# Projections beside PV issued as four column groups in one transformer layer

## The chip, the core and the metric

The kernel runs on one core of one Trainium2 chip. The metric is the device time of the kernel in microseconds (us), as the median of several runs. A difference is told against the kernel before, in per cent. The core has a matrix engine (PE, whose weight loads the profile lists apart as PEld), an elementwise engine (DVE), an activation engine (ACT), a general engine (POOL), a queue engine (SP) and 16 DMA engines. They run side by side and wait for each other through semaphores.

## The reference

One layer of 2048 rows and width 1024: an attention block with 32 query heads of 32 columns that share one key head and one value head, and a gated feed-forward block of width 3584. Each block stands behind a layer norm and is added to its input. All data are bf16.

```python
def attention(x, wq, wk, wv, wo):            # S = 2048, D = 1024, 32 heads of 32
    q = (x @ wq).reshape(B, S, 32, 32).transpose(0, 2, 1, 3)
    k, v = x @ wk, x @ wv                    # 32 columns each, shared by all heads
    p = softmax(einsum("bhqd,bkd->bhqk", q, k) * 32 ** -0.5)
    return einsum("bhqk,bkd->bhqd", p, v).transpose(0, 2, 1, 3).reshape(B, S, D) @ wo

def feed_forward(x, w_gate, w_up, w_down):   # F = 3584
    return (sigmoid(x @ w_gate) * (x @ w_up)) @ w_down

h = x + attention(layernorm(x), wq, wk, wv, wo)
out = h + feed_forward(layernorm(h), w_gate, w_up, w_down)
```

## The kernel before

**Three kinds of work on PE, three tilings of its array.** A score burst ("S", lines 685 and 695) multiplies keys by queries. The contraction is only 32 long, so four matmuls stand side by side in four row groups of the array (`tile_position=(DH * j, 0)`, form 32*128 in the profile). PV (line 842 for most of the run, 965 and 968 in the first chunk) multiplies the values by the exponentials. The stationary operand has only 32 columns, so four matmuls stand side by side in four column groups (`tile_position=(0, DH * j)`, form 128*32). The sums of the exponentials over the keys (lines 881, 894 and 947) have the tiling of PV, with ones as weights. Everything else uses the whole array (form 128*128): the Q, K and V projections and the output projection (`mm_list`, line 334), gate and up (`half_items`, line 1180) and down (`down_group`, line 1250). The document calls this third kind "f", as the code does (`kind="f"`), and calls a run of one kind between two others a stretch.

**The bursts.** Rows come in 16 tiles of 128, two tiles make a unit, and there are 8 units. The attention of a row tile is cut into quads (`ORDER`), and each quad into 8 bursts. In all there are `NB` = 512 bursts. A burst fills four banks of PSUM, and ACT empties them with two exponentials of 128x1024. Three pairs of banks (`S_ps`) are passed around. The other two banks (`X_ps`) take everything else, one group at a time in each: a group of PV has 8 items, each of four matmuls with 512 columns, and a group of f has as many items as its sum has terms. For every two groups of PV there is a group of sums with one item (`sum_group`, held in `pv_follow` until it is taken up).

**Who sets the order.** The program is written out by a planner in Python. It keeps a clock for each engine (`k_pe` and others), adds to it an estimated cost for each instruction and `T_SW` = 0.1 whenever the kind of work changes (`mode`), and picks the next item from the loop at the end of the kernel. In this order: a burst, if its banks are free by the planner's clock (`due`); an item of a PV group that has been started; output projections that are urgent; a new PV group, if its exponentials have been issued (`pv_ready`) and a burst was just made; else an item of the current f group (`cur`). So the time between two bursts, a gap, is filled with PV and f. The table `PV_PLAN` has a letter for each of the 64 quads: `a` puts off the start of a PV group while the current f group has under 1.0 left; `c` and `e` start it behind the next burst; `d` and `e` let a burst wait for the end of a PV group; a capital takes up the group of sums at once. Where the next item of PV waits for an exponential, the loop takes an item of f instead if the wait is over 0.25 by the clock (`2.5 * T_SW`, when the last kind was PV) or over 0.02 (otherwise).

**The f groups by size.** Gate and up take the weights as stationary operand and the rows as moving operand: 256 rows when both tiles of a unit are ready, 128 when only the first is (`first_tile`, whose second tile follows as a step of its own, for which the weights are loaded once more unless they are held). Down, the output projection and most of Q have 512 columns. The weights of gate and up are streamed from memory for each unit into the slots of `halves`, by SP's queue.

**Before the main loop.** A written-out head (`HEAD`) covers the first 72 us with the first projections and the first PV groups. The change is switched on where the loop starts.

Of the kernel before, what the change touches and what calls it, by code (L numbers as in the profile page):

```python
# [12 lines left out]
P = 128  # L13
DH = 32
# [70 lines left out]
def bass_sequential_preLN__grouped_kv_mqa__glu_gated_glu__prompt_kernel(  # L85
# [15 lines left out]
    DT = D // P  # L101
    NT = S // P
    KT = S // P
    NQ = D // P
    QC = 256
    NQC = S // QC
    TPQ = QC // P
    NFT = F // P
# [3 lines left out]
    BPG = KT // 2  # L112
    NB = NQC * NQ * BPG
# [2 lines left out]
    HR = 4  # L116
    NGU = 4
    NEAR = 1
    PV_PLAN = "aaaaAeAaaeaaaeaAaebabaaAdaddaaaAdababaaadabadaaCdabadaaEcaaaacaa"
    WO_PLAN = "aaaaaaba"  # L120
    PV_HOLD = 1.0
    BANK_WAIT = 0.15
# [11 lines left out]
    T_MM, T_FIX, T_SW, T_EXP, T_TANH, T_ADD = 0.0004167, 0.00267, 0.1, 0.91, 0.48, 0.61  # L134
# [4 lines left out]
    with ExitStack() as es:  # L139
# [6 lines left out]
        QT = sb("QT", [NQ, S])  # L146
# [26 lines left out]
        k_pe, k_dve, k_act, k_pool, k_sp, k_dma = [0.0], [0.0], [0.0], [0.0], [0.0], [0.0]  # L173
# [8 lines left out]
        c_pool, c_s, c_e, c_pv = ctr("c_pool", k_pool), ctr("c_s", k_pe), ctr("c_e", k_act), ctr("c_pv", k_pe)  # L182
# [18 lines left out]
        wd = zv(0, [NFT, D])  # L201
# [22 lines left out]
        hact = hact_flat[:].rearrange("p (a b) -> p a b", a=NFT)  # L224
# [14 lines left out]
        def _(unused):  # L239
# [48 lines left out]
            pe_mode = [None]  # L288

            def mode(m):  # L290
                if pe_mode[0] != m:
                    k_pe[0] += T_SW
                    pe_mode[0] = m
# [5 lines left out]
            def open_group(g):  # L299
# [3 lines left out]
                need(pe, f(True) if callable(f) else f)  # L303
                bank_free[b] = "open"

            def run_item(g):
                if g.bank is None:
                    need(pe, *[v() if callable(v) else v for v in g.after])
                    open_group(g)
                mode(g.kind)  # L310
                fn = g.items.popleft()[1]
                tick = fn(X_ps[:, g.bank, :])
                if not g.items:
                    dve_fill(when(tick) + g.room)
                    bank_free[g.bank] = g.evac(X_ps[:, g.bank, :], tick)
# [12 lines left out]
            def mm_list(pairs, sel, n):  # L328

                items = []  # L330
                last = len(pairs) - 1
                for i, (a, b) in enumerate(pairs):
                    def f(bank, i=i, a=a, b=b):
                        ins = pe.matmul(sel(bank), lhsT=a, rhs=b, start=(i == 0), stop=(i == last))  # L334
                        return mm_done(ins, n, i == last)
                    items.append((n * T_MM + T_FIX, f))
                return items
# [338 lines left out]
            def s_burst(k):  # L676
                g, b = quad(k), burst(k)[2]
                t, i = ORDER[g]
                mode("s")
                need(pe, (c_e, 2 * k - 1) if k > 0 else None, k_val[key_tile(g, b) // 2 if wide(g) else b],  # L680
                     *q_ready(g), *(xnT_ready(0, 1) if k < 2 else ()))
                if wide(g):
                    kt = key_tile(g, b)
                    for j in range(4):
                        ins = pe.matmul(S_ps[:, ((2 * k + j // 2) % 3) * 2 + j % 2, :],  # L685
                                        lhsT=kT4[DH * j:DH * (j + 1), kt * P:(kt + 1) * P],
                                        rhs=QT[DH * j:DH * (j + 1), i // 2 * 4:i // 2 * 4 + 4, t * P:(t + 1) * P],
                                        start=True, stop=True, tile_position=(DH * j, 0))
                        if j % 2 == 1:
                            c_s.inc(ins, 0.109, 0.3)  # L690
                    return
                for kt in range(2):
                    for j in range(4):
                        bank = ((2 * k + j // 2) % 3) * 2 + j % 2
                        ins = pe.matmul(S_ps[:, bank, kt * QC:(kt + 1) * QC],  # L695
                                        lhsT=kT4[DH * j:DH * (j + 1), (2 * b + kt) * P:(2 * b + kt + 1) * P],
                                        rhs=QT[DH * j:DH * (j + 1), 2 * i:2 * i + 2, t * P:(t + 1) * P],
                                        start=True, stop=True, tile_position=(DH * j, 0))
                        if kt == 1 and j % 2 == 1:
                            c_s.inc(ins, 0.115, 0.3)  # L700
# [469 lines left out]
            def half_items(n, w):  # L1170
                c, ts, fs, _ = steps[n]
                us, r0, m = step_halves(n, w), ts[0] * P, len(ts) * P
                items = []
                for j in range(2 * len(fs)):
                    for dt in range(DT):
                        def f(bank, j=j, dt=dt):
                            u = us[j // 2]
                            i = half_at[u]
                            need(pe, half_val[u])
                            ins = pe.matmul(bank[:, j * m:(j + 1) * m], lhsT=halves[i][:, dt, j % 2 * P:(j % 2 + 1) * P],  # L1180
                                            rhs=QT[:, dt, r0:r0 + m], start=(dt == 0), stop=(dt == DT - 1))
                            tick = mm_done(ins, m, dt == DT - 1)
                            if j % 2 == 1 and dt == DT - 1:
                                if i > H_KT and not held(n):
                                    wd_free.append((ZONE[i - H_KT - 1], [tick]))
                                elif not held(n):
                                    half_free.append((i, [tick]))
                                if w == 1 and c < NU - 1 and j == 2 * len(fs) - 1 and ffn_list[0][0] == "down":
                                    half_free.append((4 + c, [tick]))
                                load_halves()  # L1190
                            return tick
                        items.append((m * T_MM + T_FIX, f))
                return items
# [49 lines left out]
            def down_group(c, tt, dc, lo=0, n=512):  # L1243
                t, c0 = UNITS[c][tt], dc * 512 + lo
                items = []
                for ft in range(NFT):
                    def f(bank, ft=ft):
                        f1 = ft | 1
                        need(pe, hact_val[(t, f1)])
                        ins = pe.matmul(bank[:, 0:n], lhsT=hact[:, ft, tt * P:(tt + 1) * P],  # L1250
                                        rhs=wd[:, ft, c0:c0 + n], start=(ft == 0), stop=(ft == NFT - 1))
                        return mm_done(ins, n, ft == NFT - 1)
                    items.append((n * T_MM + T_FIX, f))

                def evac(bank, tick):
                    i = oi[0]
                    oi[0] += 1
                    need(dve, tick)
                    hv = hx[:, t % HR, c0:c0 + n]
                    v = c_dve.inc(dve.scalar_tensor_tensor(out=hv, in0=bank[:, 0:n], scalar=0.5, in1=hv,  # L1260
                                                           op0=ALU.mult, op1=ALU.add), 0.03 + n * 0.00113, 0.08)
                    next_x()
                    need(sp, v)
                    o_val[i] = dma(sp, of[t * P:(t + 1) * P, c0:c0 + n], hv, d_o[t % HR])
                    if dc == DC - 1:
                        if t + HR < NT:
                            x_due.append((t, o_val[i]))
                        if t == UNITS[c][-1]:
                            down_last[c] = tick
                    return v  # L1270
                assert wd_next[0] == NFP
                return _Group(items, evac, [wd_val[0]])
# [14 lines left out]
            def busy(g):  # L1287
                return g is not None and bool(g.items)
# [224 lines left out]
                                B_w_down[2 * i * P:2 * (i + 1) * P, :].rearrange("(a p) n -> p a n", p=P), d_wd, 512)  # L1513


            urg = [None]
            since_s = [0.0]
            idle = 0
            while True:
# [35 lines left out]
                    continue  # L1555
                if busy(pv[0]):
                    t_ = pv[0].items[0][2]()
                    if t_ > k_pe[0] + (2.5 * T_SW if pe_mode[0] == "pv" else 0.02):
                        if not busy(cur[0]):
                            cur[0] = next_group()  # L1560
                        if busy(cur[0]):
                            run_item(cur[0])
                            continue
                        if t_ > k_pe[0] + 0.6 and can_s:
                            k_pe[0] += 0.05
                            dve_fill(k_pe[0])
                            continue
                    run_item(pv[0])
                    continue
# [88 lines left out]
```

## Time and profile before

| what | value |
|---|---|
| median of 3 runs | 1100.33 us (1098.34 to 1101.48) |
| the profiled execution | 1100.95 us, span 1098.9 us |
| granted clock of PE | 0.997 |
| PE, matmuls | 1082.9 us busy (99%), 11612 instructions |
| ACT | 1008.4 us busy (92%), 1155 instructions |
| DVE | 899.6 us busy (82%), 1496 instructions |
| DMA | 173.34 MB, SP's queue 57.4% of 16 engines' span |

"Busy" is the union of the durations of an engine's instructions. A matmul's duration holds its way through the array, so that matmuls overlap one another and a busy PE is not one at its peak: what a matmul costs in a stream is the distance from its start to the next one's start. The timeline merges neighbouring instructions of a line and a shape into one row with its start, its length to the end of the last one, and their count. The times of starts in it are therefore what to read.

### The profile page before, as it was taken

Reading aid. Unit: us, or ns where it says so; the run is one execution under the profiler, and the core shown is the slowest. Engines: PE = TensorE matmul, PEld = TensorE weight load, DVE = VectorE, ACT = ScalarE, POOL = GpSimd, SP = SyncE. Lnnn points to the kernel's source line nnn. Section 1 sums busy time; section 2 is a strip of 40 time slices with the busy share of each in tenths; the row PEclk is TensorE's granted clock in tenths of the full one; section 3 lists DMA queues with packets and bytes.
Section 4 is the critical chain, followed back from the end, with each engine's and each line's share of the span. In section 5 each row is a group of like instructions: output and inputs, shape, how many; then the busy total and the mean of one; then the engine's idle time right before and its main releaser. Section 6 shows DMA issues by size and latency. Waiting matters only on the chain.

```text
span 1098.9 us, 27392 instructions
## 1 busy us (share of the span) xinstructions
PE 1082.9 (99%) x11612; PEld 616.4 (56%) x11612; DVE 899.6 (82%) x1496; ACT 1008.4 (92%) x1155; POOL 64.5 (6%) x136
## 2 busy tenths in 40 slices
PE   7899999999999999999999999999999999999999
PEld 5554456643666346643666346653665446653884
DVE  7759998799988889799987989898988889798311
ACT  6899999999999999999999999999999999999110
POOL 4500110010000000000000000000000000000000
PEclk9899999999999999999999999999999999999999
DMA  9743318940966539670999419670585609881660
GB/s 218 141 119 108 106 52 249 260 137 20 253 201 187 124 103 253 197 202 20 238 245 246 112 29 269 195 182 30 143 241 155 145 20 277 221 232 35 149 175 20
DMA packets 328233, 173.34 MB, mean 158 GB/s; under 512 B 39472, under 2 KB 322352, under 8 KB 328112
## 3 DMA queue, kind: packets, MB, share of 16 engines
q1 hardware_dynamic: 322304, 161.37, 57.4%
q0 software_dynamic: 2544, 9.44, 2.5%
q8 instruction: 91, 1.49, 0.6%
q10 hardware_dynamic: 3264, 0.79, 0.4%
q14 instruction: 30, 0.25, 0.1%
HBM read 159.51 MB, written 4.19 MB: 149 GB/s over the span
## 4 chain that ended last, share of the span: by engine, by line
PE 95%; ACT 2%; DVE 1%; DMA 1%; POOL 1%; issue 0%; DVEq 0%; ACTq 0%
PE X_ps L1180 38%; PE X_ps L1250 19%; PE S_ps L685 13%; PE X_ps L334 10%; PE X_ps L842 10%; PE S_ps L695 1%; PE X_ps L968 1%; ACT Pr L718 1%; PE X_ps L881 1%; DVE st L381 1%; PE X_ps L965 1%; ACT hact L718 1%; DMA zone<-zone 0%; DMA hx<-in_A_x_dram 0%; POOL sd L360 0%
## 5 line engine op out<-in xcount | busy, mean ns | idle before, releaser
L718 ACT ACTIVATE Pr<-S_ps 128x1024 bf16<-128x1024 f32 x992 | 936.0, 1112 | 4.0 <-PE S_ps L695 1.6
L768 DVE TENSOR_TENSOR pairs<-Pr 128x1024 bf16<-128x1024 bf16 x446 | 303.6, 683 | 28.4 <-ACT Pr L718 27.7
L780 DVE TENSOR_TENSOR pairs<-pairs 128x1024 bf16<-128x1024 bf16 x390 | 268.9, 689 | 11.0
L1180 PE MATMUL X_ps<-QT,wgu 128*128 128x128 bf16 (+1 forms) x2656 | 257.7, 247 | 0.7 <-issue 0.6
L1180 PEld LDWEIGHTS X_ps<-QT,wgu 128*128 128x128 bf16 x2656 | 198.4, 98 | 54.0 <-issue 35.9
L1250 PE MATMUL X_ps<-zone,hact 128*128 128x512 bf16 (+2 forms) x924 | 216.9, 374 | 0.0
L685 PE MATMUL S_ps<-QT,kT 32*128 32x512 bf16 x1792 | 176.8, 385 | 0.0
L1180 PE MATMUL X_ps<-QT 128*128 128x128 bf16 (+1 forms) x1840 | 175.8, 245 | 0.6 <-issue 0.5
L1180 PEld LDWEIGHTS X_ps<-QT 128*128 128x128 bf16 x1840 | 136.5, 98 | 33.2 <-issue 21.3
L1250 PEld LDWEIGHTS X_ps<-zone,hact 128*128 128x128 bf16 x924 | 78.8, 98 | 104.4 <-issue 30.4
L1201 ACT ACTIVATE gu<-X_ps 128x512 f32<-128x512 f32 x112 | 78.3, 699 | 45.9 <-PE X_ps L1180 45.9
L1222 DVE SCALAR_TENSOR_TENSOR hact<-gu,X_ps 128x512 bf16<-128x512 f32 x112 | 76.5, 683 | 52.4 <-PE X_ps L1180 51.7
L685 PEld LDWEIGHTS S_ps<-QT,kT 32*128 32x128 bf16 x1792 | 45.1, 91 | 129.9 <-ACT Pr L718 114.3
L842 PE MATMUL X_ps<-Pr,V 128*32 128x512 bf16 x1792 | 114.7, 381 | 0.0
L334 PE MATMUL X_ps<-zone 128*128 128x512 bf16 (+3 forms) x576 | 78.3, 281 | 4.2 <-DMA zone<-zone 2.1
L842 PEld LDWEIGHTS X_ps<-Pr,V 128*32 128x32 bf16 x1792 | 40.2, 96 | 50.8 <-issue 16.8
L334 PE MATMUL X_ps<-wo,QT 128*128 128x512 bf16 x256 | 63.5, 381 | 0.0
L334 PEld LDWEIGHTS X_ps<-zone 128*128 128x128 bf16 x576 | 39.3, 99 | 33.5 <-issue 13.9
L349 POOL CAST mean<-mv 128x1 f32<-128x1 bf16 x28 | 8.7, 309 | 817.9 <-DVE mv L1093 802.9
L1260 DVE SCALAR_TENSOR_TENSOR hx<-X_ps,hx 128x512 bf16<-128x512 f32 (+2 forms) x33 | 22.2, 672 | 24.7 <-PE X_ps L1250 24.5
L903 DVE STREAM_TRANSPOSE ols<-X_ps 128x512 f32<-128x512 f32 x28 | 20.0, 716 | 23.0 <-PE X_ps L881 21.5
L334 PEld LDWEIGHTS X_ps<-wo,QT 128*128 128x128 bf16 x256 | 22.2, 98 | 28.9 <-issue 8.5
(94 smaller groups left out, 541.7 us busy)
## 6 DMA issues: line engine op xcount, KB each, us to landing
wgu<-in_B_w_up_dram SPq DMA_DIRECT2D x81, 512.0 KB, 5.7
wgu<-in_B_w_gate_dram SPq DMA_DIRECT2D x72, 512.0 KB, 5.5
QT<-in_B_w_gate_dram SPq DMA_DIRECT2D x55, 512.0 KB, 5.8
QT<-in_B_w_up_dram SPq DMA_DIRECT2D x46, 512.0 KB, 6.0
zone<-in_B_w_down_dram POOLq DMA_DIRECT2D x14, 512.0 KB, 5.6
out_dram<-hx SPq DMA_DIRECT2D x31, 128.0 KB, 1.7
hx<-in_A_x_dram SPq DMA_DIRECT2D x15, 256.0 KB, 2.7
Pr<-in_B_w_gate_dram SPq DMA_DIRECT2D x5, 512.0 KB, 6.9
```

Of the source, the lines that this page charges most:

```text
L334: ins = pe.matmul(sel(bank), lhsT=a, rhs=b, start=(i == 0), stop=(i == last))
L685: ins = pe.matmul(S_ps[:, ((2 * k + j // 2) % 3) * 2 + j % 2, :], lhsT=kT4[DH * j:DH * (j + 1), kt * P:(kt + 1) * P], rhs=QT[DH * j:DH * ( ...
L718: c_e.inc(act.activation(out=p_tile(k, n % 2), in_=S_ps[:, 2 * pr:2 * pr + 2, :].rearrange("p a (b q) -> p (a b) q", q=QC), func=ACTF.Exp, ...
L768: slot_use[x] = c_dve.inc(dve.tensor_tensor(out=dst(x), in0=p_tile(k - 1, hh), in1=p_tile(k, hh), op=ALU.add), T_ADD, 0.08)
L780: slot_use[x] = slot_use[y] = c_dve.inc(dve.tensor_tensor(out=pairs[:, x, :], in0=pairs[:, x, :], in1=pairs[:, y, :], op=ALU.add), T_ADD, ...
L842: ins = pe.matmul(bank[DH * j:DH * (j + 1), :], lhsT=V[:, kt, :], rhs=p_tile(k, j // 2)[:, j % 2 * 2:j % 2 * 2 + 2, :], start=b == 0, stop ...
L903: free = c_dve.inc(dve.transpose(ols[:], bank), 0.75, 0.08)
L1180: ins = pe.matmul(bank[:, j * m:(j + 1) * m], lhsT=halves[i][:, dt, j % 2 * P:(j % 2 + 1) * P], rhs=QT[:, dt, r0:r0 + m], start=(dt == 0), ...
L1201: tanh_val[n] = c_act.inc(act.activation(out=slot, in_=bank, func=ACTF.Tanh, scale=0.5), T_TANH, 0.1)
L1222: gu_read[n] = c_dve.inc(dve.scalar_tensor_tensor(out=hact[:, 2 * fs[0]:2 * fs[0] + ft, r0:r0 + len(ts) * P], in0=slot.rearrange("p (a b) ...
L1250: ins = pe.matmul(bank[:, 0:n], lhsT=hact[:, ft, tt * P:(tt + 1) * P], rhs=wd[:, ft, c0:c0 + n], start=(ft == 0), stop=(ft == NFT - 1))
L1260: v = c_dve.inc(dve.scalar_tensor_tensor(out=hv, in0=bank[:, 0:n], scalar=0.5, in1=hv, op0=ALU.mult, op1=ALU.add), 0.03 + n * 0.00113, 0.08)
```

## The change

Three edits go together.

The first is in `run_item`. Before an item of f is issued, a new function `by_columns` decides whether the item is written in PV's tiling. It does so in the main loop only. If the last kind on PE was PV, it says yes as long as there are bursts to come (or a PV group is under way, or a group of sums waits). If the last kind was a burst, it says yes when a PV group is under way, a group of sums waits, or the next PV group has its exponentials. If the last kind was f on the whole array, it says no. An item for which it says yes is counted by the planner as PV work (`mode("pv")`), and the new function `mm` issues four matmuls for it, each with 32 of the 128 weight columns, to 32 of the 128 partitions of the bank, with the same moving operand. `mm` takes the place of `pe.matmul` in `mm_list`, `half_items` and `down_group`.

The second is in the loop: the wait for an exponential beyond which an item of f is put between two items of PV is 0.02 in every case.

The third is in the tables: `PV_PLAN` has other letters, and the planner's cost of half a burst is 0.113 where it was 0.109.

```diff
-    PV_PLAN = "aaaaAeAaaeaaaeaAaebabaaAdaddaaaAdababaaadabadaaCdabadaaEcaaaacaa"
+    PV_PLAN = "aaacAaaaaacaadaDaaaaadaBaaaaaaaBaaaaaacBdacaaaaAdaabaaaAcababaaa"
...
+            main = [False]
+
+            def by_columns():
+                if not main[0]:
+                    return False
+                more = busy(pv[0]) or pv_follow[0] is not None
+                if pe_mode[0] == "pv":
+                    return more or k[0] < NB
+                n = pv_next[0]
+                return pe_mode[0] == "s" and (more or n < NQC * NQ and k[0] >= min(BPG * (n + 1) + 1, NB - (n == NQC * NQ - 1)))
+
+            def mm(out, lhsT, rhs, start, stop):
+                if pe_mode[0] != "pv":
+                    return pe.matmul(out, lhsT=lhsT, rhs=rhs, start=start, stop=stop, skip_group_check=main[0])
+                for j in range(4):
+                    ins = pe.matmul(out[DH * j:DH * (j + 1)], lhsT=lhsT[:, DH * j:DH * (j + 1)], rhs=rhs, start=start,
+                                    stop=stop, tile_position=(0, DH * j), skip_group_check=True)
+                return ins
...
-                mode(g.kind)
+                mode("pv" if g.kind == "f" and by_columns() else g.kind)
...
-                        ins = pe.matmul(sel(bank), lhsT=a, rhs=b, start=(i == 0), stop=(i == last))
+                        ins = mm(sel(bank), a, b, i == 0, i == last)
...
-                            c_s.inc(ins, 0.109, 0.3)
+                            c_s.inc(ins, 0.113, 0.3)
...
-                            ins = pe.matmul(bank[:, j * m:(j + 1) * m], lhsT=halves[i][:, dt, j % 2 * P:(j % 2 + 1) * P],
-                                            rhs=QT[:, dt, r0:r0 + m], start=(dt == 0), stop=(dt == DT - 1))
+                            ins = mm(bank[:, j * m:(j + 1) * m], halves[i][:, dt, j % 2 * P:(j % 2 + 1) * P],
+                                     QT[:, dt, r0:r0 + m], dt == 0, dt == DT - 1)
...
-                        ins = pe.matmul(bank[:, 0:n], lhsT=hact[:, ft, tt * P:(tt + 1) * P],
-                                        rhs=wd[:, ft, c0:c0 + n], start=(ft == 0), stop=(ft == NFT - 1))
+                        ins = mm(bank[:, 0:n], hact[:, ft, tt * P:(tt + 1) * P], wd[:, ft, c0:c0 + n],
+                                 ft == 0, ft == NFT - 1)
...
+            main[0] = True
...
-                    if t_ > k_pe[0] + (2.5 * T_SW if pe_mode[0] == "pv" else 0.02):
+                    if t_ > k_pe[0] + 0.02:
```

## Prediction

> **What bounds the kernel now.** I read the page first: busy shares, slices, chain.
>
> ```profile
> PE 1082.9 (99%) x11612; PEld 616.4 (56%) x11612; DVE 899.6 (82%) x1496; ACT 1008.4 (92%) x1155; POOL 64.5 (6%) x136
> ...
> PE   7899999999999999999999999999999999999999
> ...
> ACT  6899999999999999999999999999999999999110
> ...
> PE 95%; ACT 2%; DVE 1%; DMA 1%; POOL 1%; issue 0%; DVEq 0%; ACTq 0%
> ```
>
> PE is on the chain for 95% of the span. ACT is full too, but only to the 37th slice: the last exponential ends at 1015 us, and what follows is PE alone, as the chain in order of time shows:
>
> ```profile
> 1024.99 47.60 PE X_ps L1180 x608
> 1072.59 24.26 PE X_ps L1250 x140
> ```
>
> So ACT sets when the attention ends, and PE sets when the kernel ends: it has 83 us of f left by then. A microsecond of PE saved before 1015 us takes f out of this tail, if there is f to bring forward.
>
> Then the timeline of PE shows what PE loses. It hardly ever waits; it pays at every change of tiling.
>
> ```profile
> 329.53 0.40 PE L685 MATMUL S_ps<-QT,kT 32*128 32x512 bf16 x4
> 329.85 1.69 PE L842 MATMUL X_ps<-Pr,V 128*32 128x512 bf16 x28
> 331.48 0.39 PE L685 MATMUL S_ps<-QT,kT 32*128 32x512 bf16 x4
> 331.80 0.40 PE L842 MATMUL X_ps<-Pr,V 128*32 128x512 bf16 x4
> 332.14 1.16 PE L1180 MATMUL X_ps<-QT 128*128 128x256 bf16 x9
> 333.23 0.40 PE L685 MATMUL S_ps<-QT,kT 32*128 32x512 bf16 x4
> 333.55 0.94 PE L1180 MATMUL X_ps<-QT 128*128 128x256 bf16 x7
> 334.33 0.82 PE L1180 MATMUL X_ps<-QT,wgu 128*128 128x256 bf16 x6
> 335.08 0.40 PE L685 MATMUL S_ps<-QT,kT 32*128 32x512 bf16 x4
> 335.42 0.40 PE L881 MATMUL X_ps<-pairs,ones 128*32 128x512 bf16 x4
> 335.76 1.70 PE L1180 MATMUL X_ps<-QT,wgu 128*128 128x256 bf16 x14
> ```
>
> Read starts. Seven items of PV take from 329.85 to 331.48: seven times 0.216 (the stream's distance) and 0.12 for the change to S. The single PV item at 331.80 is followed by f 0.34 later, 0.12 more than its 0.216. Every burst is entered and left at such a price, and every meeting of PV and f costs one more.
>
> **The change, part by part.** *Meetings that go.* Counted along PE's timeline from 72 us, where the loop starts: 78 stretches go from PV to f, 34 from f to PV. One of the 78 lies behind the last burst and stays. By the new rule f behind PV, and f between a burst and PV, is in PV's tiling, so 77 and 34 meetings vanish. Prices are medians of starts less the stream's distance. PV to f costs 116 ns, and the f matmul behind it is followed 11 ns late. Against that, leaving column groups for a burst costs 106 ns, leaving f costs 96 (the four of a group start 3 ns apart). So one meeting is worth 116 + 11 - 10 = 117 ns, and 77 of them 9.0 us. Burst, f, PV, burst costs 122 + 104 + 106 at its three borders; burst, columns, burst costs 119 + 106; 34 x 107 ns = 3.6 us. Together 12.6 us. The 2 x 512 borders of bursts stay.
>
> *What the column form costs at each size.* Laid over the order of before, the rule takes 1050 items of f: those behind or ahead of PV in its gap, those of 26 gaps in which a group of sums waits, and those of 7 gaps in which PV was ready and put off. By columns moved they are 302 of 512 or 384, 564 of 256 and 184 of 128, some 137 us of f. For 512 the row is PV itself: 0.216 for four, as f's own 0.216 for one. Cost nothing. For 256 the first chunk's PV shows it:
>
> ```profile
> 68.06 0.28 PE L965 MATMUL X_ps<-Pr,ones 128*32 128x256 bf16 x4
> 68.17 0.28 PE L968 MATMUL X_ps<-Pr,V 128*32 128x256 bf16 x4
> 68.28 0.28 PE L965 MATMUL X_ps<-Pr,ones 128*32 128x256 bf16 x4
> 68.39 0.28 PE L968 MATMUL X_ps<-Pr,V 128*32 128x256 bf16 x4
> ```
>
> Four each 0.109, with four fresh weight loads; f at 256 columns also takes 0.109. Cost nothing. For 128 columns no row has the column form. On the whole array one takes 0.056:
>
> ```profile
> 966.21 0.62 PE L1180 MATMUL X_ps<-QT,wgu 128*128 128x128 bf16 x8
> 966.66 1.11 PE L1180 MATMUL X_ps<-QT 128*128 128x128 bf16 x17
> 967.71 0.39 PE L685 MATMUL S_ps<-QT,kT 32*128 32x512 bf16 x4
> ```
>
> (25 in 1.50, less 0.096 for the change.) In columns, four matmuls and four loads have to fit into that. Bounds: 56 ns, as the pace was the moving operand's at 512 and at 256; and 109 ns, the pace at 256, if there the loads and not the moving operand set it. In the raw starts at 256 each load follows its matmul by 2 ns and the next matmul by another 2, so eight instructions go in 12 ns; that is far nearer to 56. I take 56 and no cost, and keep 184 x 53 ns = 9.8 us as the other end. If f of 128 columns fell into column gaps by its share of all f (137 of 603 us; 2048 such items lie in the loop), 465 x 53 ns = 25 us.
>
> [...]
>
> *Instructions.* 1050 items become 4200 matmuls and as many loads, 6300 instructions more. The instruction queue's 91 packets carried 27392; some 21 more come, on a queue of 0.6%. I cost it at nothing, since PE has fetched 8 per 0.109 us from 66.96 to 71.7 us without a hole. If each new packet were waited for as long as the hole of 241 ns at 293.3 us, 5 us: kept for the range.
>
> *What PE does with the time.* It must find f sooner. The planner does a unit's gate and up on its first tile alone when PE is early: 2048 items of 128 columns over seven units, half of them first tiles, 146 a unit out of 448. Being early by another 12.6 us in the last unit needs 225 more: 371, still under 448. So the work is there. Its price: two items of 56 take 2.5 ns more than one of 109. Early by c/8 of 12.6 us in unit c sums to 44 us, 790 items: 2.0 us. Some 12 more pairs of weight blocks are loaded twice, 25 MB on 173; the queues would pass from 57% to 66% of the span, below the 80% that the busiest 100 us already hold (900 to 1000).
>
> *The wait of 0.02.* The old 0.25 made PE wait inside a PV group. From 72 us on PE's starts show four holes of over 60 ns between matmuls of one kind, 0.6 us in all, none of them in PV. Between nothing and 0.6 us gain; I take nothing.
>
> *The tables.* Letters and the burst's 0.113 only move stretches. Nothing on the chain is shorter or longer: bursts keep two borders whatever the letter. The seventh quad loses its capital: one more sum item, 0.11 us. Bounds ±1.2 us, ten meetings more or fewer than in the order of before. ACT's and DVE's instructions stay the same, and an item that delays a burst stays at most 0.216 long.
>
> Sum: -12.6 + 0.1 + 2.0 = -10.5 us. On the profiled execution's 1100.95 that is 1090.4; this execution stands 0.6 over the median of 1100.33, so against the median 1089.8, say 1090.
>
> **The rivals.** *A, slower: weight loads bind at 128 columns.* Each such item takes 109 instead of 56 when it is issued by columns. For it: no row excludes it, and 256 columns would look the same. Against: loads of the four groups start 3 ns apart and last 97 ns each beside one another. With 184 items the time is 1090 + 9.8 = 1100; with 465, 1115. The gain is gone at 10.5 us / 53 ns = 198 items. Order moves with the table, so between these: I give 1105.
>
> *B, no change: the time can't be used.* PE comes early, finds neither rows nor weights and waits, so each unit still starts at ACT's pace. For it: first tiles show PE at that frontier already, and ACT is full. Against: the 83 us tail, of which the last tile's own work needs only 3.5 (output projection) + 25 (448 x 56 ns) + 24 (down); and 302 first tiles a unit to spare. It would give 1099 to 1101.
>
> *C: less column work than I count.* The new table starts PV at other places and keeps f to f. With half the meetings gone, 6 us saved, 1095.
>
> **How the numbers follow.** About 0.3% (3.3 us) is what a measurement of this kernel can tell from no change. Forecast, 1087 to 1093: 0.60. C: 0.10, faster. A: 0.18; four parts in ten of it end under 1097 (fewer items or a pace between), 0.02 within the bound, 0.09 slower. B: 0.07, same. Packets or table against it: 0.05, slower. That makes faster 0.77, same 0.09, slower 0.14. The range reaches from the forecast's lower end, less the table's 1.2, 1086, into A at 1104; the likeliest's own is 1087 to 1093.
>
> **What would show it.** Right: no border from PV to whole-array f in PE's timeline between 72 and 1015 us; f in form 128*32, with starts of groups 0.216, 0.109 and 0.056 apart; some 3000 matmuls more; the last exponential still near 1015 us and the tail behind it near 73 instead of 83. Wrong by A: groups of 128 columns over 0.08 apart. By B: idle PE before weight loads. By C: PV to f borders remain. It is also wrong if four groups that read the same moving operand are slower than PV's, which read four.

## The result: 0.8% slower

| | before | changed |
|---|---|---|
| median | 1100.9 us | 1109.91 us |
| ratio | | 1.0084 (95% interval 1.0068 to 1.0100) |
| profiled execution, its span | 1100.95, 1098.9 us | 1111.96, 1109.9 us |
| last exponential ends | 1015.5 us | 1026.9 us |
| from there to the end | 83.4 us | 83.0 us |

Two lines of the changed kernel's page (engine, busy time, instructions; then queue, packets, MB, share), and last the queue's line of the page before, show what grew. PE has 3900 matmuls and 3900 loads more and is busy for 2 us less in a span that is 11 us longer. The instruction queue brought 122 packets where it brought 91.

```profile
PE 1080.6 (97%) x15517; PEld 632.7 (57%) x15517; DVE 898.6 (81%) x1495; ACT 1009.2 (91%) x1155; POOL 65.1 (6%) x136
...
q8 instruction: 122, 2.00, 0.8%
...
q8 instruction: 91, 1.49, 0.6%
```

The meetings of PV and f are gone, as PE's timeline of the changed kernel shows (start, length, line, operation, count). Line 319 is now f on the whole array, line 321 f in column groups, line 704 a burst and line 861 PV.

```profile
331.99 0.39 PE L704 MATMUL S_ps<-QT,kT 32*128 32x512 bf16 x4
332.32 0.84 PE L321 MATMUL X_ps<-QT 128*32 128x256 bf16 x24
332.98 1.03 PE L861 MATMUL X_ps<-Pr,V 128*32 128x512 bf16 x16
333.95 0.40 PE L704 MATMUL S_ps<-QT,kT 32*128 32x512 bf16 x4
334.28 1.05 PE L861 MATMUL X_ps<-Pr,V 128*32 128x512 bf16 x16
335.15 1.05 PE L321 MATMUL X_ps<-QT,wgu 128*32 128x256 bf16 x32
```

Six items of f (24 matmuls) take from 332.32 to 332.98, 0.11 each. PV follows with no border, and four PV items end at f after 0.87 us, four times 0.216. So the form does what it should. What is new are holes like these in the same timeline:

```profile
466.34 0.24 PE L321 MATMUL X_ps<-QT,wgu 128*32 128x128 bf16 x4
466.41 0.39 PE L900 MATMUL X_ps<-pairs,ones 128*32 128x512 bf16 x4
466.62 0.39 PE L321 MATMUL X_ps<-QT,wgu 128*32 128x128 bf16 x13
468.91 2.32 PE L321 MATMUL X_ps<-QT,wgu 128*32 128x128 bf16 x80 [1.90 <-issue]
...
595.94 1.45 PE L321 MATMUL X_ps<-QT,wgu 128*32 128x128 bf16 x89
600.65 0.52 PE L321 MATMUL X_ps<-QT,wgu 128*32 128x128 bf16 x23 [3.26 <-issue]
```

PE stops in the middle of an item (after 13 matmuls, after 89) and waits for nothing that the program waits for: "issue". The span between 466.62 and 468.91 holds 3 items and a quarter; the rest, 2.06 us, is a hole. The windows of the same stretch (length, then busy time and count of PE, PEld, DVE, ACT, POOL, granted clock, DMA share, GB/s) show a second price behind it:

```profile
466.80:468.90 2.10, 0.21 (x13) 0.04 (x1) 1.29 (x2) 2.10 (x3) 0.00 (x0) 1.00 0.91 242
468.90:471.80 2.90, 2.89 (x103) 2.70 (x103) 0.41 (x1) 0.19 (x1) 0.00 (x0) 0.50 1.03 259
471.80:476.00 4.20, 4.20 (x69) 3.43 (x67) 3.74 (x7) 3.43 (x5) 0.00 (x0) 0.94 0.83 230
```

Behind the hole PE runs at a granted clock of 0.50 for 3.4 us (all of the 2.9 us of the second window and some 0.5 us of the third, whose mean is 0.94), and a 128-column item takes 0.107 instead of 0.056. In the second window ACT is busy for 0.19 of 2.9 us: the next burst comes late. With all such delays the attention ends 11 us later.

Other holes wait for something of the program: an exponential, rows, weights, or a bank that DVE has to empty (loads of line 900 waited six times, 1.8 us in all, for DVE's olp). Three of them, from the same timeline, with the releaser in the brackets:

```profile
116.57 0.40 PE L714 MATMUL S_ps<-QT,kT 32*128 32x256 bf16 x8 [0.33 <-ACT Pr L737]
...
204.37 0.27 PE L319 MATMUL X_ps<-QT,wgu 128*128 128x256 bf16 x1 [1.21 <-DMA wgu<-in_B_w_up_dram]
...
289.92 1.27 PE L319 MATMUL X_ps<-QT,wgu 128*128 128x256 bf16 x10 [0.89 <-DMA QT<-hn]
```

**The account.** From 72.3 us on, every distance between the starts of two items was split into the item's own pace (0.2159, 0.1093 or 0.0559 at 512, 256 and 128 columns, where one matmul lasts 0.38, 0.27 and 0.22 by the trace and overlaps the next), the median price of a border where the kind changes, and what is left. A rest of over 0.1 us is called a hole.

| us | before | changed | difference |
|---|---|---|---|
| items at their pace | 904.1 | 905.1 | +1.0 |
| borders | 113.0 | 101.9 | -11.1 |
| holes behind instruction packets | 0.0 | 9.7 | +9.7 |
| other holes | 2.0 | 10.0 | +8.0 |
| rests of 35 to 100 ns (nearly all half clock) | 0.3 | 3.8 | +3.5 |
| smaller rests | 4.9 | 4.8 | -0.1 |
| sum | 1024.3 | 1035.3 | +11.0 |

The third row counts holes that end 1.2 to 1.65 us behind the end of a packet of the instruction queue and lie a multiple of 256 PE instructions behind one another. There are eight, read off the trace's own records (us):

```
PE stops   resumes   hole   packet ended   resumes after
  77.00     77.40    0.29      75.77          1.63
 178.32    178.85    0.42     177.48          1.37
 183.56    184.13    0.47     182.91          1.22
 367.29    368.24    0.89     366.77          1.47
 373.15    374.43    0.96     372.88          1.57
 466.79    468.91    2.06     467.42          1.49
 593.58    594.83    1.20     593.46          1.37
 597.16    600.65    3.43     599.38          1.27
```

Each of the queue's 122 packets has 16 KB (2.00 MB in all). From each of these holes to the next PE ran 13, 1, 21, 1, 11, 15 and 1 times 256 recorded instructions (matmuls, loads and PE's own semaphore waits), to the instruction, and its 31286 records are 122.2 times 256: so I count a packet as 256 instructions of PE. None of the 24 other holes of over 0.1 us lies at such a place. For the hole that follows 373.15 the profile names ACT as the releaser, but the first load of that burst had gone at 373.47, and PE stood still behind it. In a stretch of 128-column items by columns, eight instructions go in 0.056 us and 256 in 1.8 us; no two packets of the kernel came closer than 3.43 us. So the theory was that PE runs out of instructions there ("fetch"). The rival was that the new order of work makes PE wait, whatever the tiling ("order").

### The profile page after: what moved, and what is told of

The parts are those of the page before. It is cut to its first block, busy times and chain, and to the rows that moved or that the text cites. A ratio compares the mean times of both kernels' runs of the same rounds, so it can differ in the third digit from the quotient of the medians.

```text
span 1109.9 us, 35211 instructions
## 1 busy us (share of the span) xinstructions
PE 1080.6 (97%) x15517; PEld 632.7 (57%) x15517; DVE 898.6 (81%) x1495; ACT 1009.2 (91%) x1155; POOL 65.1 (6%) x136
## 2 busy tenths in 40 slices
DMA packets 332424, 175.94 MB, mean 159 GB/s; under 512 B 39536, under 2 KB 326512, under 8 KB 332272
## 5 line engine op out<-in xcount | busy, mean ns | idle before, releaser
L319 PE MATMUL X_ps<-QT,wgu 128*128 128x128 bf16 (+1 forms) x2105 | 195.2, 244 | 2.9 <-DMA wgu<-in_B_w_up_dram 1.6
L319 PEld LDWEIGHTS X_ps<-QT,wgu 128*128 128x128 bf16 x2105 | 154.6, 98 | 38.2 <-issue 24.6
L319 PE MATMUL X_ps<-zone,hact 128*128 128x512 bf16 (+2 forms) x694 | 159.6, 372 | 0.0
L319 PE MATMUL X_ps<-QT 128*128 128x128 bf16 (+1 forms) x1517 | 139.3, 243 | 0.0
L319 PEld LDWEIGHTS X_ps<-QT 128*128 128x128 bf16 x1517 | 110.3, 99 | 21.9 <-issue 14.7
L319 PEld LDWEIGHTS X_ps<-zone,hact 128*128 128x128 bf16 x694 | 59.8, 98 | 75.5 <-issue 18.9
L321 PE MATMUL X_ps<-QT,wgu 128*32 128x256 bf16 (+1 forms) x2396 | 68.2, 257 | 9.0 <-issue 9.0
L321 PEld LDWEIGHTS X_ps<-QT,wgu 128*32 128x32 bf16 x2396 | 52.8, 99 | 22.3 <-issue 18.2
L319 PE MATMUL X_ps<-zone 128*128 128x128 bf16 (+3 forms) x510 | 62.3, 272 | 2.5 <-ACT QT L621 1.3
L321 PE MATMUL X_ps<-zone,hact 128*32 128x512 bf16 x920 | 58.0, 380 | 0.1
```

What stands on the lines that cost most here:

```text
L319: return pe.matmul(out, lhsT=lhsT, rhs=rhs, start=start, stop=stop, skip_group_check=main[0])
L321: ins = pe.matmul(out[DH * j:DH * (j + 1)], lhsT=lhsT[:, DH * j:DH * (j + 1)], rhs=rhs, start=start, stop=stop, tile_position=(0, DH * j), ...
```

## Experiments

### One size of item off the column form, order kept

`whole128` issues exactly the order of the changed kernel, and only the 128-column items go over the whole array.

```diff
-                if pe_mode[0] != "pv":
+                if pe_mode[0] != "pv" or n == 128:
```

> The order of work is exactly that of the changed kernel; only the items of 128 columns that it issued by columns (377 of them) go over the whole array again, so 2300 matmuls and as many loads fewer are fetched. Theory 'instruction fetch' (PE runs dry behind the instruction packets where it eats eight instructions per 56 ns): the holes that end 1.2 to 1.6 us after an instruction packet (417 + 466 + 889 + 2064 + 1195 + 3427 ns in the changed kernel) and the half clock behind the two longest (3.5 us) go nearly all, 11 us; 28 borders between PV's tiling and the whole array come back, 3 us. Time near 1110 - 11 + 3 = 1102 us. Rival 'order' (the new table makes PE wait for rows, weights and exponentials, whatever the tiling): the holes stay, 1110 + 3 = 1113 us.

Measured: 1101.82 us, 1.0010 of before (0.9999 to 1.0021), 8 us under the changed kernel. The stretch that stood still from 466.8 us is now this (timeline of `whole128`):

```profile
471.20 0.40 PE L704 MATMUL S_ps<-QT,kT 32*128 32x512 bf16 x4
471.53 0.29 PE L319 MATMUL X_ps<-QT 128*128 128x128 bf16 x2
471.65 1.06 PE L319 MATMUL X_ps<-QT,wgu 128*128 128x128 bf16 x16
472.91 1.07 PE L319 MATMUL X_ps<-QT 128*128 128x128 bf16 x16 [0.20 <-DMA QT<-in_B_w_up_dram]
```

The hole is gone, and PE keeps its pace of 0.056 an item. Borders came back for 2.8 us (104.7 against 101.9). Three holes behind packets remain clear of doubt, 2.5 us, at 256 columns (78.8, 185.2 and 431.8 us; the one at 185.2 is in whole-array code behind a stretch by columns). This is the fetch theory's number within 0.2 us; the order theory's 1113 is out.

### The order of the changed kernel without any column form

```diff
-                if pe_mode[0] != "pv":
+                if pe_mode[0] != "pv" or True:
```

> The order of work is exactly that of the changed kernel, but every item of f goes over the whole array, so the column form is gone and the order alone is left. Borders between PV and f come back, 133 of them for some 15 us by the prices of the kernel before (122 us of borders against 107). Theory 'instruction fetch': holes behind instruction packets and half clock go, 12 us; 1110 + 15 - 12 = 1113 us, with only the 11 us of holes left that wait for rows, weights, exponentials and the like. Rival 'order': 1110 + 15 = 1125 us.

Measured: 1105.89 us, 1.0047 (1.0030 to 1.0063); 92 packets, no long hole behind any. The order theory's 1125 is far off. But my 1113 was 7 us too high as well: I put the borders that return on top of all waits, and a later PE waits less for the others. In its trace the other holes come to some 6 us where the changed kernel has 10.0 (an estimate, as some matmul records are missing there). What it shows by itself is that the new order, run without the form for which it was planned, costs 5 us.

### The rate of instructions doubled, order kept

`split256` writes a gate or up item of 256 columns, when it goes by columns, as two halves. Both halves of an item's first product carry the start flag, and the output is 0.11 off (relative; the cause is not shown). No product is left out of PE's work.

```diff
-                            ins = mm(bank[:, j * m:(j + 1) * m], halves[i][:, dt, j % 2 * P:(j % 2 + 1) * P],
-                                     QT[:, dt, r0:r0 + m], dt == 0, dt == DT - 1)
+                            cut = P if m == 2 * P and pe_mode[0] == "pv" else m
+                            for o_ in range(0, m, cut):
+                                ins = mm(bank[:, j * m + o_:j * m + o_ + cut], halves[i][:, dt, j % 2 * P:(j % 2 + 1) * P],
+                                         QT[:, dt, r0 + o_:r0 + o_ + cut], dt == 0, dt == DT - 1)
```

> The order of the changed kernel; gate and up items of 256 columns that go by columns are written as two halves of 128 columns, eight matmuls and eight loads for what were four and four. Array time is 2 x 55.9 for 109.3 ns, 1.5 us over some 580 items. What doubles is the rate at which instructions are eaten there: sixteen per 0.112 us. Theory 'instruction fetch': the 256-column stretches now starve like the 128-column ones, at least the 12 us of those over again: 1122 us or more, with new holes that end about 1.2 to 1.6 us behind an instruction packet. Rival 'order': 1110 + 1.5 = 1112 us.

Measured: 1158.41 us, 1.0527 (1.0504 to 1.0550), 48.5 us over the changed kernel for 1.5 us of array time. Its holes behind packets come to over 45 us (an estimate, as some matmul records are missing), where the changed kernel has 9.7. Now the 256-column stretches stand still, as its timeline shows:

```profile
590.81 0.72 PE L321 MATMUL X_ps<-QT,wgu 128*32 128x128 bf16 x38
594.19 0.79 PE L321 MATMUL X_ps<-QT,wgu 128*32 128x128 bf16 x42 [2.66 <-issue]
```

### Instructions alone, without any column form

`cut128` takes the kernel before in its own order and cuts each gate and up item of 128 columns into four of 32 columns over the whole array: eight instructions an item, as by columns.

```diff
-                            ins = pe.matmul(bank[:, j * m:(j + 1) * m], lhsT=halves[i][:, dt, j % 2 * P:(j % 2 + 1) * P],
-                                            rhs=QT[:, dt, r0:r0 + m], start=(dt == 0), stop=(dt == DT - 1))
+                            cut = DH if m == P else m
+                            for o_ in range(0, m, cut):
+                                ins = pe.matmul(bank[:, j * m + o_:j * m + o_ + cut], lhsT=halves[i][:, dt, j % 2 * P:(j % 2 + 1) * P],
+                                                rhs=QT[:, dt, r0 + o_:r0 + o_ + cut], start=(dt == 0 and o_ == 0), stop=(dt == DT - 1),
+                                                skip_group_check=True)
```

> The kernel before in its own order, without any column form; each gate and up item of 128 columns is cut into four of 32 columns over the whole array, so it takes eight instructions as a column item does. In the head of the kernel before, whole-array matmuls of 32 columns follow one another by 25 ns, so an item takes at least 100 ns instead of 56: 2432 items, 107 us more. Theory 'instruction fetch' (PE gets its instructions in packets of 256, and the packets came no closer than 3.43 us in any run so far): 256 instructions would be eaten in 3.2 us, so in long stretches of these items, the last 384 above all, PE runs dry without any column form: packets some 3.4 us apart or more, an item 107 ns or more on average, holes at packets. Rival 'the column form itself holds PE up': 25 ns starts throughout, packets 3.2 us apart, no holes; about 1208 us.

Measured: 1256.37 us in one run, 48 us over the 1208 of the rival. Its timeline behind the attention, where PE has only these items to do:

```profile
1164.65 1.06 PE L1182 MATMUL X_ps<-QT,wgu 128*128 128x32 bf16 x36 [1.54 <-issue]
1165.56 2.56 PE L1182 MATMUL X_ps<-QT 128*128 128x32 bf16 x91
1169.75 1.15 PE L1182 MATMUL X_ps<-QT 128*128 128x32 bf16 x37 [1.63 <-issue]
1170.73 1.87 PE L1182 MATMUL X_ps<-QT,kT 128*128 128x32 bf16 x64
1172.44 0.85 PE L1182 MATMUL X_ps<-QT 128*128 128x32 bf16 x27
1175.39 3.54 PE L1182 MATMUL X_ps<-QT 128*128 128x32 bf16 x128 [2.11 <-issue]
```

36 + 91 is 127 matmuls (PE's semaphore waits fill this block up), 37 + 64 + 27 is 128, and then 128 again: after each 256 recorded instructions, loads and semaphore waits among them, PE stands still. From the hole at 1162.93 to that at 1197.05 seven such blocks took 34.1 us, 4.9 us each, where 128 matmuls 25 ns apart take 3.2. No column tiling and no burst is in this stretch, and no wait of the program at its holes. That settles what the "issue" holes in the middle of a stretch are: PE at the end of a packet.

It does not settle when a packet is late. Just ahead of this stretch the same code ran three blocks of 3.2 us with no hole between them. These windows of the same trace hold the last two of the three and the first block of the stretch:

```profile
1156.60:1159.80 3.20, 3.20 (x135) 3.20 (x131) 0.59 (x2) 0.56 (x1) 0.00 (x0) 1.00 0.45 87
1159.80:1163.00 3.20, 3.20 (x133) 3.20 (x128) 0.56 (x1) 0.04 (x1) 0.00 (x0) 1.00 0.90 254
1163.00:1168.00 5.00, 3.46 (x132) 3.36 (x128) 0.13 (x1) 0.56 (x1) 0.00 (x0) 0.80 1.17 292
```

The DMA share, the last figure but one, rises from 0.45 to 1.17 as the holes begin. From 72 us on PE ate 49 blocks of 256 instructions of `cut128` in under 4.2 us each. Where the other queues kept the DMA engines busy for under 0.6 of the time between two packets (17 blocks), the hole behind the block was under 0.1 us on average; at 0.6 to 0.9 (23 blocks) it was 0.88, at 0.9 or more (9 blocks) 1.65. So packets that have to share the DMA engines with the weights are a likely reason for late ones. This is a correlation within one run, much weaker in the changed kernel's few holes, and no run takes the weights' traffic away.

### The tables alone, and the form under the old tables

`tables` is the kernel before with the new `PV_PLAN`, the burst cost of 0.113 and the wait of 0.02. `oldtables` is the changed kernel with the three of before. The planner's own clock at the end stands in the expectations.

> The kernel before with the other PV_PLAN, the burst cost of 0.113 and the wait of 0.02; no item goes by columns. The planner's own clock ends at 1104.1 where that of the kernel before ends at 1088.4. Theory 'the table fits one plan only' (letters were fitted to the plan with columns and are a loss without them): before's chip time stands 12.5 us over its plan; 1104.1 + 12.5 less 4.1 us (1024 half bursts counted 0.004 too dear) = 1112 us. Rival 'letters only move stretches' (as predicted): 1100 us, within 1.2.

> Columns at any size as in the changed kernel, with the PV_PLAN, burst cost and wait of the kernel before. The planner's clock ends at 1094.7, 8.7 us behind that of the changed kernel. Theory 'fetch, and plan': 1094.7 + 12.5 as in the kernel before, + 10 to 13 us of holes behind instruction packets and half clock = 1117 to 1120 us. Rival 'the new table is what costs': with the old one the time falls to 1100 or below, as 12 us of borders go and nothing comes.

Measured: `tables` 1113.60 us, 1.0129 (1.0107 to 1.0151); `oldtables` 1127.12 us, 1.0237 (1.0199 to 1.0275). So the letters don't "only move stretches": the three tables, fitted to one plan and put on another, cost 13 to 17 us. In the trace of `tables` holes that are not at packets come to some 12 us, where the kernel before has 2.0. `oldtables` is 7 us over the upper end of what I expected, and part of its 17 us is fetch again: its profiled execution, at 1120.19 the shortest of the four, has holes behind packets of 2.2 us at 686.4, 1.8 at 813.5 and 1.7 at 216.1. Its longest hole, 2.9 us at 129.9, waits for rows (DVE's QT).

### The change without 128 columns, planned as such

`no128` tells the planner to leave 128-column items on the whole array, and counts half a burst at 0.109. `best256` is the same with letters fitted to it.

```diff
-                mode("pv" if g.kind == "f" and by_columns() else g.kind)
+                mode("pv" if g.kind == "f" and g.items[0][0] > 0.08 and by_columns() else g.kind)
...
-    PV_PLAN = "aaacAaaaaacaadaDaaaaadaBaaaaaaaBaaaaaacBdacaaaaAdaabaaaAcababaaa"
+    PV_PLAN = "aaacAaaaaaEaDaaAaaCaaabBBaCaAbaBaBabaaaAaaaabaaBaaaDaAaaaaBBdAad"
```

> The changed kernel's rule and table, but an item of 128 columns is always written for the whole array, and the order is planned with that known; burst cost 0.109. The planner's clock ends at 1085.8, 2.6 us before that of the kernel before. Theory 'fetch': no hole over 1 us behind an instruction packet but perhaps one or two at 256 columns (1 to 3 us): 1085.8 + 12.5 + 2 = 1100 us, so the change without its 128-column part is level with before, 1098 to 1102. Rival 'waits for rows, weights and exponentials are what costs': 1106 us or more, as in the run with the whole array.

> The rule with 128-column items always on the whole array, burst cost 0.109, and a PV_PLAN fitted to this rule by some 10000 plans (the planner's clock ends at 1083.1; 1088.4 for the kernel before, 1085.8 for the run no128). Theory 'plan and fetch': 1083.1 + 12.5, and 1 to 3 us of holes behind packets at 256 columns: 1097 to 1099 us, 0.2 to 0.3% under the kernel before. Rival 'the plan's clock says nothing within 5 us': anywhere from 1095 to 1106.

> The kernel before, unchanged but for a PV_PLAN fitted to it anew with as many plans (the planner's clock ends at 1087.6, 0.8 us under that of the kernel before). It shows what fitting the letters alone gives. Theory 'plan and fetch': 1099.5 us, 0.8 less than before. Rival: a fitted table alone gives as much as the run best256.

Measured: `no128` 1100.52 us, 1.0003 (0.9991 to 1.0014). `best256` 1099.12 us, 0.9977 (0.9968 to 0.9986), faster than before by 0.23%. `beforetable`, the kernel before with letters fitted anew, 1101.73 us, 1.0001 (0.9991 to 1.0012). So there is a gain in the form, but a small one. The account of `best256` by the same split: borders 103.7 (-9.3 against before), items +1.0, holes behind packets 2.3, other holes 6.0 (+4.0), rests of 35 to 100 ns +0.6 (its loop has no stretch of half clock). Its last exponential ends at 1014.3 and the tail is 83.2 us.

## Why the prediction was wrong, step by step

- **Meetings that go.** Right: -12.6 us forecast, -11.1 measured. The borders of all kinds fall from 1081 to 970, by the 111 that were counted, and one single border from PV to whole-array f is left from 72 us on.
- **The column form at each size.** Right at all three, and rival A is out: starts of groups are 0.216, 0.109 and 0.056 apart, the last being the one for which no row existed. Rival A had 0.109 for it.
- **Instructions: the step that failed.** I costed them "at nothing" and bounded them at 5 us; holes behind packets took 9.7 us and the half clock behind the two longest another 3.5 us. The count was low as well: 374 items of 128 columns went by columns where I had 184, and 31 packets were added where I had 21. The 91 packets did not carry all engines' 27392 instructions, as I read it, but PE's alone: its 23477 records are 91.7 times 256, and 31286 in the changed kernel are 122.2 times 256, with 122 packets. The proof of cover was too short: the stretch from 66.96 to 71.7 us has some 300 instructions, hardly more than one packet, so it could not show a rate that lasts. `no128` has a hole of 1.9 us in just that kind of code (first-chunk PV at 74.8 us). And the bound had the wrong unit: most packets cost nothing, and one that is late costs up to 3.4 us. What I should have compared is the 1.8 us in which 256 instructions are eaten with the distance of packets, 3.46 us at the least in the kernel before.
- **What PE does with the time.** Wrong in the main. "So the work is there" did not come to pass: 64 items of 256 columns became pairs of 128 where I had put 790, and the new order has 10.0 us of other holes where before had 2.0. PE waits for weights, rows and exponentials. Rival B, which had 0.07, is up to a good third of what I left out. `best256`, whose loop has only 2.3 us of holes behind packets, shows its size: of 9.3 us of borders 4.0 came back as waits.
- **Where the gain would show.** Wrong: the tail did not shrink (83.4 us before, 83.0 in the changed kernel, 83.2 in `best256`). The bursts' times moved instead. The bytes agree that hardly any f was brought forward: the kernel moves 175.94 MB where it moved 173.34, and I had counted 25 MB of second loads as the price.
- **The tables.** Wrong: "bounds ±1.2 us" against +13 us for the new table on the old plan. I counted borders and not what order does to waits.
- **The sum.** -11.1 + 1.0 is near my -10.5; what I left out is +21 (9.7 + 3.5 + 8.0). Rival C has no part in it.

What stays open: why single holes differ so much (0.3 to 3.4 us), that is, what sets when the next packet comes and how far the weights' traffic delays it; and how much of the 8 us of other holes follows from the late bursts themselves. I did not try to separate these.

## What to carry to other kernels

Splitting items into narrower matmuls took PE from 11612 matmuls and as many loads to 15517 of each here, and the packets that bring them came no closer than 3.43 us in the changed kernel; compare the time in which the code eats a packet's 256 with the distance of packets before calling more instructions free. In these runs code that ate them in 1.8 to 3.5 us stood still at some packets (for 0.3 to 3.4 us in the changed kernel), in `cut128` above all where the DMA engines were full (a share of 0.90 to 1.17 from 1159.8 to 1168.0 us). The kernels without the column form (`before`, `whole`), whose 128-column items take 7 us for 256 instructions (128 times 0.056), had no long hole at a packet. And a table fitted to one plan is part of that plan: compare a change with its own fit on both sides, and look for the time saved on a full engine among the waits for whatever feeds it (in `best256` 4.0 of 9.3 us).

## What the runs showed of the hardware that I had not expected

- Four column groups of 128 moving columns, with four fresh loads, follow one another by 56 ns in the changed kernel, as its whole-array matmuls of 128 columns do (medians).
- PE's instructions came in packets of 16 KB, about one for every 256 of its records (122 packets for 31286 in the changed kernel, 91 for 23477 in the kernel before). In the eleven profiled runs no two came closer than 3.32 us. In the long starved stretch of `cut128` a block of 256 took 4.9 us on average, and at its start the DMA share was 1.17. At the eight holes of the changed kernel PE resumed 1.22 to 1.63 us behind the end of a packet.
- In the changed kernel the granted clock fell to 0.50 for 3.4 us behind a hole of 2.1 us (from 468.9 us), and again for 3.4 us behind one of 3.4 us (from 602.0 us). It did not fall behind every hole of about that length: one of 1.9 us at 74.8 in `no128` left it at 1.00.
